# The first batch's filter in 74 small transfers beside x, and the weights behind x in one queue

## The chip, the cores and the metric

The kernel runs on one core of a Trainium2 chip. A core has five engines that run side by side: TensorE (PE: the matmuls, with PEld for its weight loads), VectorE (DVE), ScalarE (ACT), GpSimd (POOL) and SyncE (SP, which only issues transfers here). Transfers between the chip's memory and the on-chip memory are issued by SyncE, ScalarE or GpSimd, each in the order of its own program, and are carried out by 16 DMA engines that all the queues share. The metric is the device time in microseconds (us) from the first to the last instruction. It is taken as a median over runs, lower is better.

## The reference

A Fourier filter over the sequence, followed by a two-layer network with an ELU:

```python
def _attn_ref(x, filt_r, filt_i):          # x: (8, 3008, 256)
    X = np.fft.rfft(x, axis=1)             # 1505 frequencies
    Y = X * (filt_r + 1j * filt_i)[None]   # filt_r, filt_i: (1505, 256)
    return np.fft.irfft(Y, n=x.shape[1], axis=1)

def _moe_ref(x, w_in, w_out):              # x: (24064, 256)
    h = x @ w_in                           # (256, 2048)
    g = np.where(h > 0, h, np.exp(np.minimum(h, 0)) - 1)
    return g @ w_out                       # (2048, 256)
```

The two weights arrive as 64-bit floats: 2 x 256 x 2048 x 8 bytes are 8.4 MB. The filters are 32-bit: 2 x 1505 x 256 x 4 bytes are 3.08 MB. One batch of x is 3008 x 256 x 4 bytes, 3.08 MB.

## The kernel before

The sequence length is split as 3008 = 47 x 64. The work on one batch is a chain of small matrix products.

- *a*: 64-point transforms over one index. For batch 0 this is `a_first(c)` in six chunks c of four pairs of rows. It needs the chunk of x that `x_load_first(c)` brings (two transfers: 64 rows of 4 KB, and 64 times four runs of 1 KB) and a 256 KB piece of the table `tf`.
- *t*: `t_first(g)` brings the result of *a* into the layout that the next step wants, by transposing on TensorE. It needs `eye`. Batches 1 to 7 do this by a trip through memory.
- *b*: `b_unit(b, g)` for g = 0 to 7: the 47-point transforms on TensorE, then four products with the filter on VectorE (L312 to L315).
- *bi* and *y*: `bi_unit` and `y_write` are the inverse 47-point transforms and a trip through memory.
- *n*: `n_unit` is the last inverse transform. Its six pieces m per batch are the input rows of the network.

The network (`up_steps`, `down_steps`) takes each piece through four quarters of the 2048 hidden channels, with a seven-product scheme for 2 x 2 blocks, so that w_in and w_out are held in seven combinations per quarter (`w_in[q]`, `w_out[q]`).

The schedule is written out by hand. After a start-up stage, the loop over `items` (8 batches, 6 pieces, 4 quarters) interleaves the network of one batch with the Fourier steps of the next, by the table `plan`. Batch 0 has no earlier batch to hide behind. So the start-up stage has to do the whole Fourier chain of batch 0 up to `n_unit(0, 0)`, and also turn the 64-bit weights into 32-bit ones. This study is about that stage.

Each of 16 weight blocks k (512 KB) takes four calls: `w_fetch(k)` issues its transfer; `w_split(k)` (VectorE, L576 and L577) takes mantissa and exponent bits apart; `w_float(k)` (ScalarE, L582 to L587) makes floats of them; `w_join(k)` (VectorE, from L593) puts them together and, for every second block, forms the three extra combinations. The blocks share buffers with x and other tiles. Blocks 0 to 7 are worked on before the first `b_unit`, blocks 8 to 15 between the steps of *b* (`TICKS`).

The filter of batch 0 is one tile `ff`, 128 x 8192 floats, of which each `b_unit(0, g)` reads the part g. Row q of the first half-tile is a frequency 64 q + ..., so neighbouring rows of the tile lie 64 KB apart in memory, in runs of 2 KB or (mirrored, read backwards) of 1 KB. `ff` is zeroed first, since some entries get no data. Every transfer into `ff` brings all eight values of g for its rows. So the first product of `b_unit(0, 0)` waits for the last of them.

The transfers of the start-up stage before the change stand in two queues:

- SyncE: table piece and x chunk for c = 0 to 5, the tables `gr`, `gi`, `gf`, `eye`, then 11 transfers of filt_r (`f_read_first(ff, a, 0)`), then `gb` and a table for *n*.
- GpSimd: weight blocks 0 and 1, the zeroing of four tiles and of `ff`, then in the loop over c a one-element copy from x chunk c into `junk` (L670; it makes the queue wait until that chunk has landed) and weight block c + 2; after it 11 transfers of filt_i (`f_read_first(ff, a, 1)`), then weight blocks 8 to 13, and 14 and 15.

In the compiled program every queue has eight semaphores for its transfers, taken in turn. From the ninth on, a transfer is issued only when the one eight before it in the same queue has landed.

Of the kernel before, what the change touches and what calls it, by code (L numbers as in the profile page):

```python
# [10 lines left out]
FP32 = mybir.dt.float32  # L11
# [11 lines left out]
N1 = 47  # L23
N2 = 64
NF = N // 2 + 1
P = 128
D = 256
# [4 lines left out]
XC = 4  # L32
NXC = H // XC
NG = K2 // 4
# [3 lines left out]
HALVES = slice(0, 64), slice(64, 128)  # L38
# [67 lines left out]
def kernel(  # L106
# [9 lines left out]
    nc = tc.nc  # L116

    ta_d, tn_d, gb_d, gr_d, gi_d, tf_d, eye_d, gf_d = [
        nc.inline_tensor(t, name=n + "_t").ap()
        for t, n in zip(_make_tables(), ("ta", "tn", "gb", "gr", "gi", "tf", "eye", "gf"))  # L120
    ]

    def pool(name, bufs, **kw):
        return ctx.enter_context(tc.tile_pool(name=name, bufs=bufs, **kw))

    glob = pool("glob", 1)
# [17 lines left out]
    gb, gr, gi = (glob.tile([P, 2, 64], FP32, name=n) for n in ("gb", "gr", "gi"))  # L144
# [1 line left out]
    w_in, w_out = ([glob.tile([P, 7, 2, P], FP32, name="%s%d" % (n, i)) for i in range(4)] for n in ("wi", "wo"))  # L146

    fbufs = [glob.tile([P, 2, 2, D], FP32, name="f%d" % i) for i in range(FBUFS)]
    junk = glob.tile([P, 1], FP32, name="junk")
    edges = glob.tile([P, 2], FP32, name="edges")  # L150
    fd = fdp.tile([NG, 2, 48, 2, 2, D], FP32, name="fd")

    xs, tas, tns, t1s, t2s, ss, t3s, t4s, zs, yds, ys, g_of, po_of, cs_, sds = ({} for _ in range(15))

    def raw(src, row, ap, col=0):
        return bass.AP(tensor=src.tensor, offset=src.offset + row * D + col, ap=ap)
# [52 lines left out]
    zt = [[], [w[3].rearrange("p a b c -> p (a b c)") for w in (w_in, w_out)]]  # L209
    ROWS = 112  # L210

    def x_load_first(c):
        if c < XBUFS:
            t = xp.tile([P, 2, 2, D], FP32, tag="xc", name="xc").rearrange("p k u d -> p (k u) d")
        else:
            t = t1p.tile([P, XC, D], FP32, tag="t1", name="x1")
        if c < 2:
            w = tnp.tile([P, 4, P], FP32, tag="tn", name="tn")
        else:
            if c % 2 == 0:  # L220
                tas["pair"] = t4p.tile([P, 4, D], FP32, tag="t4", name="t0").rearrange("p u (w f) -> p (u w) f", f=P)
            w = tas["pair"][:, 4 * (c % 2):4 * (c % 2) + 4, :]
        xs[0, c], tas[0, c] = t, w
        nc.sync.dma_start(w, tf_d[:, 4 * c:4 * c + 4, :])
        nc.sync.dma_start(t[HALVES[0]].rearrange("p u d -> p (u d)"), raw(x, XC * c, [[N1 * D, 64], [1, XC * D]]))
        u = 1 if c == 0 else 0
        if u:
            nc.gpsimd.memset(t[HALVES[1], 0, :], 0.0)
        nc.sync.dma_start(t[HALVES[1], u:XC, :], raw(x, N1 - XC * c - u, [[N1 * D, 64], [-D, XC - u], [1, D]]))

    def a_first(c):
        xt, w = xs.pop((0, c)), tas.pop((0, c))
# [44 lines left out]
        for a, r in enumerate((LO, HI)):  # L277
            nc.gpsimd.dma_start(t[r].rearrange("p c u d -> p (c u d)"), fd[g, a].rearrange("q c u d -> q (c u d)"))

    def f_read_first(t, a, part):  # L280

        r = a * 64
        for src, c, queue in (((filt_r, 0, nc.sync), (filt_i, 1, nc.gpsimd))[part],):
            queue.dma_start(t[r:r + 24, :, c, :, :].rearrange("q g u d -> q g (u d)"),
                                raw(src, 2 * a, [[64 * D, 24], [4 * D, NG], [1, 2 * D]]))
            for u in range(2):
                g0 = 1 if a == u == 0 else 0
                for r0, n in ((24, 16), (40, 7)):  # L290
                    queue.dma_start(t[r + r0:r + r0 + n, g0:NG, c, u, :],
                                        raw(src, 64 * (r0 - 23) - 4 * g0 - 2 * a - u,
                                            [[64 * D, n], [-4 * D, NG - g0], [1, D]]))
            if a == 0:
                queue.dma_start(t[24:48, 0, c, 0, :], raw(src, 32, [[64 * D, 24], [1, D]]))

    def tile_mm(ps, table, k, rhs, special):
        for u, w, v in ((0, 1, 1), (1, 1, 0)) if special else ((0, 2, 0),):
# [44 lines left out]
    def tn_read(b, m):  # L343
        w = tns[b, m] = tnp.tile([P, 4, P], FP32, tag="tn", name="tn")
        nc.sync.dma_start(w, tn_d[:, 4 * m:4 * m + 4, :])
# [200 lines left out]
    def w_fetch(k):  # L546
        q, j = divmod(k, 4)

        if k in (3, 4):
            wd = t2p.tile([P, 4, D], FP32, tag="t2", name="wd").rearrange("p u d -> p (u d)")  # L550
        elif k in (10, 11):
            wd = t1p.tile([P, XC, D], FP32, tag="t1", name="wd").rearrange("p u d -> p (u d)")
        elif k in (6, 7, 8, 9, 15):
            wd = xp.tile([P, 2, 2, D], FP32, tag="xc", name="wd").rearrange("p k u d -> p (k u d)")
        else:
            wd = fbufs[{5: 0, 12: 1, 13: 2, 14: 0}.get(k, k)].rearrange("p c u d -> p (c u d)")
        wd = wds[k] = wd.bitcast(U32).rearrange("p (a w) -> p a w", w=2)
        if j < 2:
            srcs = [moe_w_in.bitcast(U32)[ts(j, P), ts(q, 1024)]]
        else:  # L560
            srcs = [moe_w_out.bitcast(U32)[ts(4 * q + 2 * (j - 2) + i, P), :] for i in range(2)]
        for i, s in enumerate(srcs):
            n = 512 // len(srcs)
            nc.gpsimd.dma_start(wd[:, ts(i, n), :].rearrange("p a w -> p (a w)"), s)

# [65 lines left out]
    with tc.manual_schedule():  # L633
# [3 lines left out]
        with tc.tile_pool(name="boot", bufs=1) as bp:  # L637
            ff = bp.tile([P, NG, 2, 2, D], FP32, name="ff")
            eye = bp.tile([P, P], FP32, name="eye")
            gf = bp.tile([P, 2, 64], FP32, name="gf")  # L640
            pq = [bp.tile([P, 2, D], FP32, name="pq%d" % i) for i in range(2)]
            zt[0] += [bp.tile([P, 16 * ROWS], FP32, name="zt%d" % i) for i in range(2)]

            for k in range(2):
                w_fetch(k)
            for c in range(NXC):
                x_load_first(c)
            wtmp.append([kp.tile([P, 512], U32, tag=t, name=n) for t, n in (("k0", "wm"), ("k1", "we"))] +
                        [kp.tile([P, 2, 512], FP32, tag="c", name="wfl")])
            wtmp.append([sdp.tile([P, 2, D], FP32, tag="sd", name=n).bitcast(U32).rearrange("p a b -> p (a b)")  # L650
                         for n in ("wm", "we")] +
                        [t1p.tile([P, XC, D], FP32, tag="t1", name="wfl").rearrange("p (a b) d -> p a (b d)", a=2)])
            for i, v in enumerate((1151.0 * 2 ** 23, 255.0 * 2 ** 23)):
                nc.vector.memset(edges[:, i:i + 1], v)
            for z in zt[0] + zt[1]:
                nc.gpsimd.memset(z.rearrange("p (k r) -> p k r", r=ROWS)[:, :, 48:64], 0.0)
            nc.gpsimd.memset(ff, 0.0)
            for t, d in ((gr, gr_d), (gi, gi_d), (gf, gf_d), (eye, eye_d)):
                nc.sync.dma_start(t, d)
            for a in range(2):  # L660
                f_read_first(ff, a, 0)

            def tick(k):
                w_float(k)
                w_join(k - 1)

            for c in range(NXC):
                w_split(c)

                nc.gpsimd.tensor_copy(out=junk[0:1], in_=xs[0, c][0:1, 0, 0:1])  # L670
                w_fetch(c + 2)
                w_float(c)
                a_first(c)
                if c > 0:
                    w_join(c - 1)
            for a in range(2):
                f_read_first(ff, a, 1)
            for k in range(NXC + 2, 14):
                w_fetch(k)
            for g in range(4):  # L680
                t_first(g)
            for k in range(NXC, 8):
                w_split(k)
                tick(k)
                w_fetch(8 + k)
            nc.sync.dma_start(gb, gb_d)
            tn_read(0, 0)
            for g in range(NG + 2):
                k = TICKS.get(g)
                if k:  # L690
                    w_split(k)
                if 2 <= g < NG - 2:
                    t_first(g + 2)
                if g >= 2:
                    bi_unit(0, g - 2)
                if g < NG:
                    b_unit(0, g, ff[:, g], gf, pq if g % 2 else None)
                if g >= 2:
                    y_write(0, g - 2, (nc.sync, nc.scalar if g == NG + 1 else nc.sync))
                if g == NG + 1:  # L700
                    y_read(0, 0, (nc.sync, nc.scalar))
                if k:
                    tick(k)
# [22 lines left out]
        for b in range(B):  # L726
            t = (b - 1) * PER
            if b > 0:
# [7 lines left out]
                for g in range(NG + 2):  # L736
                    s = t + 9 + g
# [6 lines left out]
                for g in range(NG):  # L744
                    s = t + 7 + g
# [11 lines left out]
        for i in range(-PER, len(items) + 3):  # L757
# [3 lines left out]
            for k in "UUDUDDU":  # L761
                s = ups if k == "U" else downs
# [4 lines left out]
            for k in "DUUDUDD":  # L767
                s = ups if k == "U" else downs
# [40 lines left out]
```

## Time and profile before

| | before |
|---|---|
| time, median of 3 | 2679.97 us (2678.12 to 2680.19) |
| profiled span | 2675.4 us |
| TensorE busy | 2597.6 us (97%) |
| VectorE busy | 1841.1 us (69%) |
| ScalarE busy | 1504.4 us (56%) |
| GpSimd busy | 252.2 us (9%) |
| first matmul of the last inverse transform of batch 0 (L363) | 125.5 us after the start |

TensorE is busy nearly all the time from about 126 us on. Before that it has gaps, and the rows of the profile that matter are those of the first 126 us: which transfer ends which wait, and how much the 16 DMA engines move in each stretch. A stretch's row gives the busy time of each engine and its count of instructions, the granted TensorE clock, the mean busy share of the DMA engines (transfers that overlap on one engine can take it above 1) and the GB/s moved.

### The profile page before, as it was taken

The numbers are of one execution on the slowest core, as the hardware profiler recorded it, in microseconds if no ns is written. First come the engines' busy times: TensorE is split into PE (matmuls) and PEld (weight loads), VectorE is DVE, ScalarE is ACT, GpSimd is POOL, SyncE is SP. The second block draws the span as 40 slices with busy tenths as digits, with TensorE's granted clock in tenths as the row PEclk, the third lists the DMA queues.
The fourth block names the chain that finished last, engine by engine and source line by source line (L and its number), as shares of the span: only waits on it lengthen the run. The fifth ranks groups of instructions, "written<-read, shape, count | busy, mean of one in ns | idle before, by whom it ended". The sixth has DMA issues, their size and how long they took to land.

```text
span 2675.4 us, 37291 instructions
## 1 busy us (share of the span) xinstructions
PE 2597.6 (97%) x13508; PEld 2213.8 (83%) x13508; DVE 1841.1 (69%) x3201; ACT 1504.4 (56%) x2621; POOL 252.2 (9%) x302
## 2 busy tenths in 40 slices
PE   3699999999999999999999999999999999999998
PEld 3388789887898878988789878898789887898887
DVE  3876766767766776767766776676767677666665
ACT  4565555655555555555555555555555555555554
POOL 3030200012000120002100021000210011000000
PEclk7799999999999999999999999999999999999999
DMA  9564421343114331343314233133421233110110
GB/s 194 145 143 100 112 50 38 90 104 97 38 45 120 86 85 35 82 104 79 77 43 102 73 97 75 38 85 97 103 56 38 73 83 85 38 40 19 22 26 16
DMA packets 230936, 202.87 MB, mean 76 GB/s; under 512 B 132952, under 2 KB 197579, under 8 KB 230753
## 3 DMA queue, kind: packets, MB, share of 16 engines
q1 hardware_dynamic: 213457, 164.84, 25.5%
q0 software_dynamic: 16992, 35.19, 5.5%
q8 instruction: 107, 1.75, 0.3%
q14 instruction: 76, 0.62, 0.1%
q10 hardware_dynamic: 304, 0.46, 0.1%
HBM read 128.45 MB, written 74.97 MB: 76 GB/s over the span
## 4 chain that ended last, share of the span: by engine, by line
PE 95%; DMA 3%; DVE 2%; ACT 0%; issue 0%; SPq 0%; POOL 0%; DVEq 0%; POOLq 0%; ACTq 0%
PE po L493 42%; PE phs L411 25%; PE phd L411 12%; PE pha L411 6%; PE psn L363 3%; PE pva L300 2%; PE psr L300 2%; PE psa L201 2%; DMA wd<-in_moe_w_out_dram 1%; DMA ff<-in_filt_i_dram 1%; DMA xc<-in_x_dram 1%; DMA tn<-tf_t 0%; PE pvb L300 0%; PE psa L236 0%; PE psi L300 0%
## 5 line engine op out<-in xcount | busy, mean ns | idle before, releaser
L493 PE MATMUL po<-g,wo 128*128 128x256 f32 (+1 forms) x5376 | 1297.1, 376 | 0.0
L493 PEld LDWEIGHTS po<-g,wo 128*128 128x128 f32 x5376 | 1016.7, 190 | 127.9 <-issue 16.2
L422 ACT ACTIVATE g<-phs 128x512 f32<-128x512 f32 (+1 forms) x576 | 338.7, 588 | 843.3 <-PE phs L411 842.6
L419 DVE TENSOR_TENSOR g<-phd,g 128x512 f32<-128x512 f32 (+1 forms) x384 | 259.4, 676 | 464.9 <-ACT e L429 278.7
L429 ACT ACTIVATE e<-e 128x512 f32<-128x512 f32 (+1 forms) x768 | 477.3, 621 | 24.3
L411 PE MATMUL phs<-y,wi 128*128 128x256 f32 (+1 forms) x1536 | 395.0, 380 | 0.0
L411 PE MATMUL phs<-ys,wi 128*128 128x256 f32 (+1 forms) x1536 | 387.8, 375 | 1.5 <-ACT g L422 1.5
L433 DVE SCALAR_TENSOR_TENSOR g<-e,g 128x512 f32<-128x512 f32 (+1 forms) x576 | 386.9, 672 | 0.2 <-ACT e L429 0.2
L428 ACT ACTIVATE e<-g 128x512 f32<-128x512 f32 (+1 forms) x576 | 352.9, 613 | 35.1 <-DVE g L419 29.0
L411 PEld LDWEIGHTS phs<-y,wi 128*128 128x128 f32 x1536 | 285.0, 190 | 82.7 <-ACT t L332 34.1
L411 PEld LDWEIGHTS phs<-ys,wi 128*128 128x128 f32 x1536 | 291.9, 190 | 34.8 <-ACT g L422 2.2
L433 DVE SCALAR_TENSOR_TENSOR g<-e,phs 128x512 f32<-128x512 f32 (+1 forms) x192 | 129.9, 677 | 138.4 <-ACT e L429 138.4
L411 PE MATMUL phd<-ys,wi 128*128 128x256 f32 (+1 forms) x768 | 194.0, 375 | 1.8 <-DVE g L419 1.8
L411 PE MATMUL pha<-y,wi 128*128 128x256 f32 (+1 forms) x768 | 193.9, 375 | 0.0
L411 PE MATMUL phd<-y,wi 128*128 128x256 f32 (+1 forms) x768 | 193.7, 375 | 0.0
L428 ACT ACTIVATE e<-phs 128x512 f32<-128x512 f32 (+1 forms) x192 | 112.9, 588 | 141.9 <-PE phs L411 141.0
L321 POOL TENSOR_TENSOR sr<-sr,sp 128x512 f32<-128x512 f32 x56 | 71.2, 1271 | 1242.8 <-DVE sp L314 1242.8
L411 PEld LDWEIGHTS phd<-ys,wi 128*128 128x128 f32 x768 | 145.9, 190 | 18.7 <-DVE g L419 2.5
L411 PEld LDWEIGHTS pha<-y,wi 128*128 128x128 f32 x768 | 146.0, 190 | 16.6 <-ACT y L365 0.2
L411 PEld LDWEIGHTS phd<-y,wi 128*128 128x128 f32 x768 | 146.1, 190 | 16.2
L473 DVE TENSOR_TENSOR g<-g,g 128x512 f32<-128x512 f32 (+1 forms) x192 | 130.7, 681 | 6.7
L470 DVE TENSOR_TENSOR g<-g,g 128x512 f32<-128x512 f32 (+1 forms) x192 | 130.7, 681 | 6.6
(141 smaller groups left out, 2403.0 us busy)
## 6 DMA issues: line engine op xcount, KB each, us to landing
yd<-t SPq DMA_DIRECT2D x127, 192.0 KB
t<-yd SPq DMA_DIRECT2D x190, 128.0 KB
z<-t SPq DMA_DIRECT2D x84, 256.0 KB
f<-fd POOLq DMA_DIRECT2D x112, 192.0 KB, 3.7
t<-z SPq DMA_DIRECT2D x224, 96.0 KB
out_dram<-o SPq DMA_DIRECT2D x640, 32.0 KB
tn<-tn_t SPq DMA_DIRECT2D x48, 256.0 KB
xc<-in_x_dram SPq DMA_DIRECT2D x84, 128.0 KB
```

Of the source, the lines that this page charges most:

```text
L300: nc.tensor.matmul(ps[:, u:u + w, :], table[k, v, :], r[k, u:u + w, :], start=n == 0, stop=n == len(rhs) - 1)
L321: nc.gpsimd.tensor_tensor(out=sr, in0=sr, in1=p, op=ALU.add)
L363: nc.tensor.matmul(ps[:, ts(q, P)], t[:, i - 4 * m, ds(dh * P, P)], w[:, i - 4 * m, :], start=True, stop=True)
L411: nc.tensor.matmul(ps[:, a, 0:h], w_in[q][:, COMBO[n], a, :], y[n], start=start and a == 0, stop=True, skip_group_check=True)
L419: nc.vector.tensor_tensor(out=g[o], in0=i0, in1=i1, op=ALU.add)
L422: nc.scalar.activation(out=g[o], in_=i0, func=AXT.Copy)
L428: nc.scalar.activation(out=e, in_=src, func=AXT.Relu, scale=-1.0)
L429: nc.scalar.activation(out=e, in_=e, func=AXT.Exp, scale=-1.0)
L433: nc.vector.scalar_tensor_tensor(out=g[n], in0=es[n], scalar=1.0, in1=src, op0=ALU.subtract, op1=ALU.max)
L470: nc.vector.tensor_tensor(out=b12, in0=b22, in1=b12, op=ALU.subtract)
L473: nc.vector.tensor_tensor(out=g["t4"], in0=g["b21"], in1=g["t2"], op=ALU.subtract)
L493: nc.tensor.matmul(po[i][:, u, 0:h], w_out[q][:, COMBO[n], a, :], g[n][:, a, :], start=q == 0 and a == 0 and n in (1, 3, 6, 4), stop=True, ...
```

## The change

The filter of batch 0 no longer waits behind x and the weights. It goes out from GpSimd's queue from the start, both filters, cut into pieces of four rows: 6 groups of rows x 2 half-tiles x 2 filters x 3 transfers, and 2 single ones, 74 in all where there were 22. GpSimd does not issue any weights any more. They go into SyncE's queue, between the chunks of x: x chunk, table piece, weight blocks, in the order in which they are needed. The `junk` copy that paced GpSimd's queue goes. `x_load_first` is split into `x_place_first` (which takes the buffers) and the issue of the transfers, and the table piece now follows its x chunk. Since GpSimd is to issue at once, `ff` is zeroed by ScalarE (one half) and VectorE (the other).

```diff
-    def x_load_first(c):
+    def x_place_first(c):
...
-        nc.sync.dma_start(w, tf_d[:, 4 * c:4 * c + 4, :])
-        nc.sync.dma_start(t[HALVES[0]].rearrange("p u d -> p (u d)"), raw(x, XC * c, [[N1 * D, 64], [1, XC * D]]))
+
+    def x_load_first(c):
+        t = xs[0, c]
         u = 1 if c == 0 else 0
         if u:
             nc.gpsimd.memset(t[HALVES[1], 0, :], 0.0)
+        nc.sync.dma_start(t[HALVES[0]].rearrange("p u d -> p (u d)"), raw(x, XC * c, [[N1 * D, 64], [1, XC * D]]))
         nc.sync.dma_start(t[HALVES[1], u:XC, :], raw(x, N1 - XC * c - u, [[N1 * D, 64], [-D, XC - u], [1, D]]))
+        nc.sync.dma_start(tas[0, c], tf_d[:, 4 * c:4 * c + 4, :])
...
-    def f_read_first(t, a, part):
...
-        r = a * 64
-        for src, c, queue in (((filt_r, 0, nc.sync), (filt_i, 1, nc.gpsimd))[part],):
-            queue.dma_start(t[r:r + 24, :, c, :, :].rearrange("q g u d -> q g (u d)"),
-                                raw(src, 2 * a, [[64 * D, 24], [4 * D, NG], [1, 2 * D]]))
-            for u in range(2):
-                g0 = 1 if a == u == 0 else 0
-                for r0, n in ((24, 16), (40, 7)):
-                    queue.dma_start(t[r + r0:r + r0 + n, g0:NG, c, u, :],
-                                        raw(src, 64 * (r0 - 23) - 4 * g0 - 2 * a - u,
-                                            [[64 * D, n], [-4 * D, NG - g0], [1, D]]))
-            if a == 0:
-                queue.dma_start(t[24:48, 0, c, 0, :], raw(src, 32, [[64 * D, 24], [1, D]]))
+    def f_read_first(t):
...
+        for q in range(0, 24, 4):
+            for a in range(2):
+                for c, src in enumerate((filt_r, filt_i)):
+                    r = 64 * a + q
+                    nc.gpsimd.dma_start(t[r:r + 4, :, c, :, :].rearrange("q g u d -> q g (u d)"),
+                                        raw(src, 64 * q + 2 * a, [[64 * D, 4], [4 * D, NG], [1, 2 * D]]))
+                    n = min(4, 23 - q)
+                    for u in range(2):
+                        g0 = 1 if a == u == 0 else 0
+                        nc.gpsimd.dma_start(t[r + 24:r + 24 + n, g0:NG, c, u, :],
+                                            raw(src, 64 * (q + 1) - 4 * g0 - 2 * a - u,
+                                                [[64 * D, n], [-4 * D, NG - g0], [1, D]]))
+        for c, src in enumerate((filt_r, filt_i)):
+            nc.gpsimd.dma_start(t[24:48, 0, c, 0, :], raw(src, 32, [[64 * D, 24], [1, D]]))
...
-            nc.gpsimd.dma_start(wd[:, ts(i, n), :].rearrange("p a w -> p (a w)"), s)
+            nc.sync.dma_start(wd[:, ts(i, n), :].rearrange("p a w -> p (a w)"), s)
...
-            for k in range(2):
-                w_fetch(k)
             for c in range(NXC):
+                x_place_first(c)
+            for c in range(3):
                 x_load_first(c)
+                for k in ((0, 1), (2,), (3,))[c]:
+                    w_fetch(k)
+            nc.scalar.memzero(ff[:, 0:NG // 2])
...
-            nc.gpsimd.memset(ff, 0.0)
-            for t, d in ((gr, gr_d), (gi, gi_d), (gf, gf_d), (eye, eye_d)):
-                nc.sync.dma_start(t, d)
-            for a in range(2):
-                f_read_first(ff, a, 0)
+            nc.vector.memset(ff[:, NG // 2:NG], 0.0)
+            f_read_first(ff)
...
             for c in range(NXC):
                 w_split(c)
-
-                nc.gpsimd.tensor_copy(out=junk[0:1], in_=xs[0, c][0:1, 0, 0:1])
-                w_fetch(c + 2)
                 w_float(c)
                 a_first(c)
                 if c > 0:
                     w_join(c - 1)
-            for a in range(2):
-                f_read_first(ff, a, 1)
-            for k in range(NXC + 2, 14):
+                if c + 3 < NXC:
+                    x_load_first(c + 3)
+                if c + 3 == NXC:
+                    for t, d in ((gr, gr_d), (gi, gi_d), (gf, gf_d), (eye, eye_d)):
+                        nc.sync.dma_start(t, d)
+                w_fetch(c + 4)
+            for k in range(NXC + 4, 14):
                 w_fetch(k)
```

More of the change, by code (lines that the diff above doesn't have):

```diff
@@ L148 @@
     fbufs = [glob.tile([P, 2, 2, D], FP32, name="f%d" % i) for i in range(FBUFS)]
-    junk = glob.tile([P, 1], FP32, name="junk")
     edges = glob.tile([P, 2], FP32, name="edges")
```

## The prediction

> **What bounds the kernel now.** I first looked at the busy shares by stage. The columns are: stretch in us, its length, busy us of PE, PEld, DVE, ACT, POOL, granted clock, DMA share, GB/s.
>
> ```profile
> 5.00:36.00 31.00, 16.37 (x80) 15.19 (x80) 17.07 (x35) 19.12 (x42) 13.87 (x19) 0.89 1.06 250
> 36.00:66.00 30.00, 10.23 (x76) 8.62 (x76) 8.91 (x18) 11.90 (x23) 8.98 (x16) 0.67 1.01 145
> 66.00:75.00 9.00, 0.00 (x0) 0.00 (x0) 1.25 (x3) 0.66 (x1) 3.22 (x6) 0.50 1.01 335
> 75.00:113.00 38.00, 34.80 (x197) 14.04 (x198) 36.86 (x74) 25.26 (x44) 0.52 (x1) 0.84 0.31 86
> 113.00:126.00 13.00, 2.45 (x16) 1.11 (x15) 9.88 (x21) 6.73 (x12) 0.00 (x0) 0.70 0.56 136
> 126.00:2675.00 2549.00, 2533.72 (x13144) 2174.87 (x13142) 1767.02 (x3053) 1439.42 (x2500) 221.78 (x250) 1.00 0.29 71
> ```
>
> The reader is to see three regimes. From 126 us TensorE is the bound (2533.7 of 2549 us) and nothing in the change touches that. From 75 to 113 us VectorE is (36.9 of 38 us): the filter products of batch 0 and weight blocks 8 to 15. Up to 75 us it is the DMA engines, whose share is about 1, and the compute engines stand still towards the end of it. In that part the rate is 250 GB/s while x and weights move, 145 while the filter moves, 335 once only weights are left.
>
> The waits of VectorE and the chain of waits say which transfer ends the stage:
>
> ```profile
> DVE sr L312 <- DMA ff<-in_filt_r_dram: 23.2, 1, 23.2
> ```
>
> ```profile
> 13.19 14.02 DMA xc<-in_x_dram
> ...
> 34.48 12.48 DMA wd<-in_moe_w_out_dram
> ...
> 47.24 16.84 DMA ff<-in_filt_i_dram
> ...
> 65.24 9.10 DMA wd<-in_moe_w_out_dram
> ...
> 74.35 0.68 DVE si L313
> ```
>
> VectorE is idle for 23.2 us and starts the first product (L312) at 73.75 us, released by a filt_r transfer of SyncE's queue. The chain names weights just before 74.35, but L313 reads no weights. GpSimd's timeline shows that filt_i was in before that:
>
> ```profile
> 53.99 0.58 POOL L291 DMA_DIRECT2D ff<-in_filt_i_dram  x1 [1.18 <-DMA ff<-in_filt_i_dram]
> 56.19 0.58 POOL L564 DMA_DIRECT2D wd<-in_moe_w_in_dram  x1 [1.61 <-DMA ff<-in_filt_i_dram]
> ...
> 68.43 0.53 POOL L564 DMA_DIRECT2D f<-in_moe_w_in_dram  x1 [0.42 <-issue]
> ```
>
> The last filt_i transfer leaves at 53.99 us. The issue at 68.43 waits for it (it is eight places on), so it landed by then. Its operands have long been ready: *b*'s first matmuls run at 44.9 us. So the start-up could be up to 73.75 - 50.5 = 23.2 us shorter at an unchanged later course, 50.5 us being where VectorE has finished weight block 6.
>
> [...] the share is about 1 from 5 to 75 us whichever queue feeds. So the change can gain from order, evenness and packet mix, not from a second road. [...]
>
> **The change part by part.**
>
> *Bytes.* Before the first product VectorE needs x (3.1 MB), six pieces of `tf` (1.5 MB), weight blocks 0 to 7 (4.2 MB), small tables (0.3 MB) and the whole filter (3.1 MB): 12.2 MB, the same before and after. Blocks 8 to 15 (4.2 MB) now come behind them. Before, blocks 8 to 10 and part of 11 to 13 came ahead of the end of the filter: in 0 to 74 us about 0.7 + 250 x 31 = 7.8 MB, 145 x 30 = 4.4 MB and 8 us at 335 = 2.7 MB were moved, 15 MB. So 2.8 MB leave the stage.
>
> *DMA time.* x, tables and weights, 9.1 MB, at the 250 GB/s of the first row: 36 us. The filter: if it moves at 145 GB/s even when spread out, 21 us; if it is only slow because much of it is in flight at once, and runs at 250 beside x, 12 us. With 2 us until the first bytes: 50 to 59 us. I take 57, since nothing in the trace shows the filter fast.
>
> *GpSimd's queue.* It can't issue before `ff` is zeroed. GpSimd's own zeroing of 8192 columns takes 6.92 us (3.94 to 10.86). ScalarE gets 4096 columns; its 512-column operations take about 0.6 us, so at most 4.8 us after the table load that ends at 2.03, thus 6.9 us. VectorE gets the other half from about 1 us; its 512-column operations take 0.42 us, so 3.4 us. Both are hidden: the first weights, which ScalarE and VectorE wait for, land at 9.2 us before, and now behind the first x chunk. GpSimd starts at about 6.5 us. One issue costs 0.53 to 0.58 us (L564 and the smaller L291), so 74 are 39 to 43 us. From the ninth on each also waits for the landing of the one eight before: 74 / 8 = 9.25 round trips. The trace bounds a round trip from both sides: 3.7 us is the median of f<-fd (192 KB, DMA share about 0.3), and 10.4 us is the median for the `fd` tile, whose transfers stand behind large ones. That makes 34 or 96 us. I estimate 3.2 us fixed (3.7 less 192 KB at 375 GB/s) plus the queueing: [...] That is 5.8 us, and 9.25 x 5.8 = 54 us. The filter is complete at about 6.5 + 52 = 58 to 60 us.
>
> *SyncE's queue.* x chunk 5 now stands behind 7.6 MB and its share of the filter. By the same rates it lands at about 45 to 49 us, later than before, where the last `a_first` starts at 36.28. From that start to *b*'s first matmul it took 44.88 - 36.28 = 8.6 us, so *b* is ready at 54 to 58 us. Block 7 lands near 57; `w_split(7)` and `w_join(6)` (0.84 and 2.1 us of VectorE) come before the first product: 60 us. Waits for buffers in the queue (block 5 for `w_join(0)`, 6 to 9 for `a_first(0)` to `(3)`) are over before their turn. Behind them stand only later blocks, `gb` and y_write, whose first issue was at 82 us.
>
> *Removed.* The `junk` copies and the pacing cost nothing but order.
>
> *Sum.* First product at about 60 us instead of 73.75. After it the same 52 us follow: VectorE is busy 36.9 of 38 us with unchanged work, and blocks 8 to 15 arrive at 335 GB/s, 1.6 us each, against 5 us per step that uses them. So the gain reaches the end one for one: 2680 - 14 = 2666 us.
>
> **Rivals.**
>
> *A, quicker.* The filter runs at x's rate when spread out, everything is there at 50 us, and the first product starts at 51 to 54: 20 to 23 us, 2657 to 2660. For it: 335 GB/s at the end shows headroom. Against: each GpSimd issue, 39 us at least, plus waits.
>
> *B, hidden or given back.* The round trip is 6.5 to 8 us, or x starves behind 4 KB filter packets: first product at 69 to 78 us, within 5 us of now, 2675 to 2685. For it: weights from GpSimd took 7 us to land at best.
>
> *C, slower.* [...] their round trip is near 10.4 us: complete at 6.5 + 96 = 102 us, and 28 us are lost: 2708. With 9 us it is 90 and 2696. For it: only a few rows per transfer, landings of 13.8 to 18.7 us for `ff` now. Against: those are of transfers five times as large behind half-megabyte blocks.
>
> **How the numbers follow.** My case, first product between 54 and 69 us: 0.65, of which I expect 60. A: 0.13. B: 0.10. C: 0.12. Faster is my case and A, 0.78. The range goes from 2655 (A with nothing lost) to 2684 (B), which leaves out C and a little beyond A.
>
> **What would show it.** Right: L312 first starts near 60 us, its wait is a few us, GpSimd's 74 issues end by about 55 us with under 0.3 us between most, GB/s is above 200 from 5 to 57 us, and from the first product to L363's first matmul there are 52 us as before. Wrong: GpSimd stands 0.5 us or more before most issues; the filter's last transfer is the releaser at over 70 us; x chunk 5 lands after 55 us; or the stage after the first product grows because blocks 8 to 15 come late.

## The result, and the profile after

The changed kernel takes 2716.3 us (median of 4 runs, 2714.7 to 2720.9), beside 2679.1 us for the kernel before on the same chip: a ratio of 1.0142, 95% interval 1.0124 to 1.0159. It is 37 us slower. The forecast was 2666 us.

First, the busy shares by stage of the changed kernel. The columns are those of the table in the prediction: stretch, length, busy us of PE, PEld, DVE, ACT and POOL with counts, granted clock, DMA share, GB/s.

```profile
5.00:15.00 10.00, 3.50 (x16) 3.34 (x16) 3.70 (x8) 6.66 (x13) 5.08 (x8) 0.90 1.02 253
15.00:65.00 50.00, 19.77 (x88) 18.58 (x89) 17.97 (x39) 16.89 (x38) 19.13 (x32) 0.57 1.11 155
65.00:95.00 30.00, 7.06 (x54) 5.59 (x52) 3.21 (x8) 9.40 (x17) 13.08 (x22) 0.61 1.07 171
95.00:110.00 15.00, 0.00 (x0) 0.00 (x0) 0.00 (x0) 0.00 (x0) 6.91 (x12) 0.50 0.35 51
110.00:149.00 39.00, 33.54 (x194) 13.89 (x195) 37.44 (x74) 25.28 (x44) 0.52 (x1) 0.84 0.24 61
149.00:163.00 14.00, 2.67 (x16) 0.94 (x16) 10.82 (x23) 6.89 (x12) 0.00 (x0) 0.76 0.54 127
163.00:2713.00 2550.00, 2534.45 (x13144) 2172.38 (x13144) 1766.96 (x3053) 1439.87 (x2500) 222.71 (x250) 1.00 0.29 71
```

The long TensorE stage is the same (2534.45 busy us of 2550, before 2533.72 of 2549), and so is the VectorE stage ahead of it. All that grew is the start-up: it lasted until 74 us before the change and now lasts until 110. In it the DMA share is as high as ever (1.11), but the rate is 155 GB/s where it had been 250 in the first 36 us. The engines are occupied and move less: a share of 1 doesn't say that bytes flow. From 95 to 110 us no compute engine does anything, and GpSimd issues 12 transfers.

The waits of the changed kernel name what is missing. The columns are engine, tile, line, releaser: us in total, times, longest.

```profile
DVE sr L315 <- DMA ff<-in_filt_r_dram: 36.0, 1, 36.0
...
POOL ff L294 <- DMA ff<-in_filt_r_dram: 33.3, 18, 5.0
...
POOL ff L294 <- DMA ff<-in_filt_i_dram: 17.9, 14, 2.7
```

VectorE stands 36.0 us before its first product (L315, which was L312) and is released by the filter. Ahead of that GpSimd itself stands for its own transfers' landings, 33.3 + 17.9 us over these 32 issues. The chain of waits (start, us, what) shows how landing follows landing:

```profile
5.99 0.78 POOL ff L289
6.77 9.88 DMA ff<-in_filt_r_dram
...
16.93 11.51 DMA ff<-in_filt_i_dram
...
29.42 12.74 DMA ff<-in_filt_r_dram
...
92.20 12.42 DMA ff<-in_filt_r_dram
...
107.17 3.23 DMA ff<-in_filt_r_dram
```

GpSimd begins at 5.99 us. Then one transfer of 10 to 13 us after another lies on the chain, each of which lets GpSimd issue the one eight places on. The part on issues says the same (out<-in, engine, operation, count, KB each, median us from issue to landing):

```profile
ff<-in_filt_r_dram POOLq DMA_DIRECT2D x12, 64.0 KB, 12.2
...
ff<-in_filt_r_dram POOLq DMA_DIRECT2D x15, 32.0 KB, 11.8
```

A piece of 64 KB lands in 12.2 us, and one of half the size in 11.8. The median of all 74 is 11.5 us, and 74 / 8 x 11.5 = 106 us, which from the first issue at 6 us on leads to 112; VectorE was released at 110.

The timelines show the other operands of the first product (start, us, engine, line, what, in brackets the idle time before it and its releaser):

```profile
56.39 3.76 PE L238 MATMUL psa<-t,x 128*128 128x128 f32 x16 [6.76 <-DMA t<-tf_t]
...
67.53 0.43 DVE L579 TENSOR_SCALAR wm<-wd 128x512 uint32<-128x512 uint32 x1 [2.13 <-DMA wd<-in_moe_w_out_dram]
...
110.49 0.69 DVE L315 TENSOR_TENSOR sr<-psr,ff 128x512 f32<-128x512 f32 x1 [35.97 <-DMA ff<-in_filt_r_dram]
```

The last `a_first` starts at 56.39 us (before 36.28), weight block 7 is split at 67.53, and VectorE has no more to do at 74.5. So x and weights are late too, by 20 us in the case of x. That lateness is hidden: VectorE is through with it 36 us before the filter is there. From the first product to *n*'s first matmul it takes 52.4 us (162.9 - 110.5; before 51.7). The 36.7 us lost by the first product reach the end one for one.

### The profile page after: what moved, and what is told of

It reads as the page before. It is cut to its first block, busy times and chain, and to the rows that moved or that the text cites. A ratio compares the mean times of both kernels' runs of the same rounds, so it can differ in the third digit from the quotient of the medians.

```text
span 2713.3 us, 37327 instructions
## 1 busy us (share of the span) xinstructions
PE 2601.0 (96%) x13508; PEld 2214.7 (82%) x13508; DVE 1843.5 (68%) x3202; ACT 1509.2 (56%) x2622; POOL 269.0 (10%) x334
## 4 chain that ended last, share of the span: by engine, by line
PE 93%; DMA 4%; DVE 2%; ACT 0%; issue 0%; POOL 0%; DVEq 0%; ACTq 0%
PE po L496 42%; PE phs L414 24%; PE phd L414 12%; PE pha L414 6%; PE psn L366 3%; DMA ff<-in_filt_r_dram 2%; PE pva L303 2%; PE psr L303 2%; PE psa L200 2%; DMA ff<-in_filt_i_dram 1%; DVE si L316 0%; DVE sr L315 0%; PE pvb L303 0%; DMA t<-yd 0%; DVE wfl L598 0%
## 5 line engine op out<-in xcount | busy, mean ns | idle before, releaser
L414 PEld LDWEIGHTS phd<-y,wi 128*128 128x128 f32 x768 | 145.8, 190 | 16.5
```

The source lines that it names most:

```text
L414: nc.tensor.matmul(ps[:, a, 0:h], w_in[q][:, COMBO[n], a, :], y[n], start=start and a == 0, stop=True, skip_group_check=True)
```

## The experiments

The filter's pieces land slowly. Four theories were to be told apart: that each transfer has a long fixed round trip, whatever its shape; that the pitch or scattering of the rows read slows them; that a piece of four neighbouring rows is too narrow, in the number of its rows ('narrow' in the expectations) or in the partitions that it writes ('port'; no view shows engines or ports of a piece, so both names are guesses); and that the order in SyncE's queue is what hurts. Some kernels below ran once only. The kernel before took 2668 to 2683 us in the runs made beside the experiments, so a single time says little about a difference of less than 15 us; the landings in its trace say more.

### Cut along g instead of along rows

Each piece now takes as many rows as the kernel before (24, 16 or 7) and two of the eight g. There are 82 of them, of 38 KB in the mean where the 74 have 42.

```diff
-        for q in range(0, 24, 4):
+        for p in range(0, NG, 2):
...
-                    nc.gpsimd.dma_start(t[r:r + 4, :, c, :, :].rearrange("q g u d -> q g (u d)"),
-                                        raw(src, 64 * q + 2 * a, [[64 * D, 4], [4 * D, NG], [1, 2 * D]]))
+                    nc.gpsimd.dma_start(t[r:r + 24, p:p + 2, c, :, :].rearrange("q g u d -> q g (u d)"),
+                                        raw(src, 4 * p + 2 * a, [[64 * D, 24], [4 * D, 2], [1, 2 * D]]))
...
```

> The changed kernel with its filter cut the other way: all 24 (16, 7) rows per transfer, but two of the eight values of g; 82 transfers of about the same size instead of 74. Theory 'narrow' [...]: the median landing falls from 11.5 us to 4 to 6 us, GpSimd issues nearly back to back, and the last filter piece lands at 55 to 65 us. Theory 'round trip' (under this load a landing takes about 11.5 us whatever the shape, and eight in flight set the rate): median landing stays at 10 to 13 us and the last piece lands at 82 / 8 x 11.5 + 6 = 124 us. Theory 'pitch' (reads 64 KB apart are slow in themselves): nothing gained or worse, 110 us or later, since now up to 24 rows of that pitch are read by one transfer. The first product needs only the pieces of its own g here, so its start alone decides nothing; the landings do.

It took 2664.5 us, ratio 0.9959 (0.9944 to 0.9974): faster than the kernel before. Its issues and its stretch from 25 to 65 us:

```profile
ff<-in_filt_r_dram POOLq DMA_DIRECT2D x8, 96.0 KB, 7.3
...
ff<-in_filt_r_dram POOLq DMA_DIRECT2D x15, 32.0 KB, 6.7
```

```profile
25.00:65.00 40.00, 25.95 (x151) 21.43 (x153) 23.82 (x50) 25.56 (x52) 24.93 (x45) 0.76 0.99 255
```

96 KB over 24 rows land in 7.3 us where 64 KB over four take 12.2. So the time isn't fixed per transfer, nor set by the bytes of a piece. The last pieces still leave only at 76.4 us, later than expected. The first product starts at 57.8 us all the same: it reads only its own g, which lands first. Two things changed at once here, the shape of a piece and the order in which the filter comes; the run with rows spread out, below, has the first alone.

### Eight rows a piece, and the old 22 pieces

```diff
-        for q in range(0, 24, 4):
+        for q in range(0, 24, 8):
...
-                    n = min(4, 23 - q)
+                    n = min(8, 23 - q)
```

> The changed kernel with pieces of eight rows, 38 transfers instead of 74. 'Round trip': the landing stays near 11.5 to 13 us, the filter is complete at 38 / 8 x 12 + 6 = 63 us, the first product at about 70 to 76 us (then weight block 7 decides), time near 2680 us. 'Narrow': [...] about the same, 60 to 65 us. 'Pitch': bytes decide, complete at 100 us or later, time near 2710 us.

The other run has the pieces of the kernel before (24, 16 and 7 rows, all g), but all from GpSimd's queue at the start:

```diff
-        for q in range(0, 24, 4):
-            for a in range(2):
-                for c, src in enumerate((filt_r, filt_i)):
-                    r = 64 * a + q
+        for a in range(2):
+            for c, src in enumerate((filt_r, filt_i)):
+                r = 64 * a
...
```

> The changed kernel with the filter in the old 22 pieces (24, 16 and 7 rows), all from GpSimd's queue from the start; the rest of the change stays. 'Round trip' and 'narrow': complete at 40 to 60 us, the first product at 65 to 75 us, time 2670 to 2682 us: the cut alone made the kernel slower. 'Pitch': complete at 90 us or later, time 2695 us or more. If x and the weights are what the early filter costs, weight block 7 lands at 67 us or later all the same.

Eight rows: 2691.6 us, ratio 1.0061 (1.0037 to 1.0085). Pieces of twice the size land in 12.7 us (median), hardly more than those of four rows, so the last leaves at 63.0 us instead of 107.7. The time is about 12 us above what was expected, since the first product starts only at 83.8 us: x and weights had become the later of the two (the last `a_first` at 68.3 us, weight block 7 split at 76.3). Old pieces: 2679.3 us, ratio 1.0015 (1.0008 to 1.0022). All 22 are issued by 39.1 us and land in 13.8, and the first product, at 72.1 us, again comes behind x and weights (last `a_first` at 60.4). So the cost of filter transfers beside x isn't only their own time, it is also what they do to x. From 25 to 65 us the run with eight rows moved:

```profile
25.00:65.00 40.00, 11.25 (x48) 10.46 (x48) 10.30 (x23) 11.41 (x24) 13.04 (x23) 0.59 1.08 149
```

### The side that is read: pitch and scattering

The first run reads the rows 63 KB apart instead of 64, the second takes a row's eight runs from one contiguous stretch. Both multiply batch 0 with other frequencies of the filter; transfers, sizes and destinations are as in the changed kernel.

```diff
-                                        raw(src, 64 * q + 2 * a, [[64 * D, 4], [4 * D, NG], [1, 2 * D]]))
+                                        raw(src, 63 * q + 2 * a, [[63 * D, 4], [4 * D, NG], [1, 2 * D]]))
...
```

> The changed kernel with its 74 pieces, but the rows of the filter of batch 0 are read 63 KB apart instead of 64 KB, so that batch 0 is multiplied with other frequencies; sizes, counts and order are unchanged. 'Pitch': the median landing falls from 11.5 to 6 us or less, the rate in 25 to 65 us rises from 150 to 220 GB/s or more, the filter is complete at 50 to 65 us, time 2665 to 2680 us. 'Narrow' and 'round trip': landing 10.5 to 12 us, complete at 100 to 108 us, time within 5 us of 2716.

```diff
-                                        raw(src, 64 * q + 2 * a, [[64 * D, 4], [4 * D, NG], [1, 2 * D]]))
+                                        raw(src, 64 * q + 2 * a, [[64 * D, 4], [2 * D, NG], [1, 2 * D]]))
...
```

> The changed kernel with its 74 pieces, but the eight runs of a row are read from one contiguous stretch (step 2 KB or 1 KB instead of 4 KB), so that batch 0 is multiplied with other frequencies; destinations, sizes and counts are unchanged. If the scattered reading in memory is what makes a four-row piece slow, its landing falls from about 12 us (64 KB pieces) to 7 or 8. 'Narrow' [...]: 11 to 12.5 us as before, filter complete at 100 to 109 us.

2712.7 us (ratio 1.0143, 1.0122 to 1.0164) and 2716.9 us (one run); first product at 106.7 and 112.2 us, landings of 11.0 and 11.9 us. Neither matters: the 64 KB pitch is cleared, as far as a change to 63 KB can clear it.

### The order without the filter

This kernel has no filter transfers for batch 0; its filter stays zero.

```diff
     def f_read_first(t):
-        for q in range(0, 24, 4):
...
+        pass
```

> The changed kernel without any filter transfer for batch 0 (its filter stays zero). It shows what x and the weights take in SyncE's queue alone. If the early filter is what holds them up: above 230 GB/s from 5 to 45 us, the last first-step matmul group begins at 34 to 42 us instead of 56.4, weight block 7 is taken at 40 to 48 us instead of 67.5, the first product starts at 48 to 56 us, time 2652 to 2665 us. If the new order in SyncE's queue is itself slow: the group begins after 50 us and the time stays above 2670.

2651.6 us (one run). The last `a_first` starts at 33.2 us, the first product at 45.9. Its windows:

```profile
15.00:25.00 10.00, 6.00 (x35) 5.58 (x36) 7.00 (x15) 7.84 (x18) 0.00 (x0) 1.00 1.07 280
25.00:35.00 10.00, 7.75 (x47) 7.20 (x46) 7.68 (x17) 6.83 (x16) 0.00 (x0) 0.66 0.99 282
```

x and weights alone run at 280 GB/s at the same DMA share. The order in SyncE's queue is innocent. Putting the filter back as in the change adds its 3.1 MB and takes the total down to 155 GB/s.

### Same pieces, rows spread out

Here a piece still has four rows, the same bytes and the same place in the queue, but its rows lie six apart: rows q, q+6, q+12, q+18, each in another group of four partitions. The count stays 74.

```diff
-        for q in range(0, 24, 4):
+        for q in range(6):
...
-                    nc.gpsimd.dma_start(t[r:r + 4, :, c, :, :].rearrange("q g u d -> q g (u d)"),
-                                        raw(src, 64 * q + 2 * a, [[64 * D, 4], [4 * D, NG], [1, 2 * D]]))
+                    nc.gpsimd.dma_start(t[r:r + 19:6, :, c, :, :].rearrange("q g u d -> q g (u d)"),
+                                        raw(src, 64 * q + 2 * a, [[6 * 64 * D, 4], [4 * D, NG], [1, 2 * D]]))
...
```

> The changed kernel with its 74 pieces of four rows, but each piece takes four rows that stand six partitions apart instead of four neighbours; the result is the same. 'Port' [...]: landing falls from 12 us to 8 or less, filter complete by 75 us. 'Narrow' [...]: unchanged, 11 to 12.5 us, complete at 100 to 109 us.

2684.4 us (one run), 32 us less than the changed kernel. Its issues, the stretch from 25 to 65 us of the changed kernel and then its own, and its first product:

```profile
ff<-in_filt_r_dram POOLq DMA_DIRECT2D x12, 64.0 KB, 7.8
...
ff<-in_filt_r_dram POOLq DMA_DIRECT2D x15, 32.0 KB, 7.5
```

```profile
25.00:65.00 40.00, 15.58 (x71) 14.52 (x71) 14.41 (x33) 13.03 (x29) 14.38 (x24) 0.54 1.11 149
```

```profile
25.00:65.00 40.00, 17.19 (x108) 14.87 (x108) 14.71 (x32) 20.65 (x42) 23.98 (x41) 0.71 1.08 259
```

```profile
76.55 0.69 DVE L313 TENSOR_TENSOR sr<-psr,ff 128x512 f32<-128x512 f32 x1 [22.63 <-DMA ff<-in_filt_r_dram]
```

12.2 us have become 7.8, the total is 259 GB/s instead of 149 in the same stretch, and the last `a_first` comes at 40.4 us. Only which rows share a piece was changed, so it isn't their number that makes a piece slow. The last piece leaves at 74.6 us, hardly earlier than with the cut by g (76.4), where the first product started at 57.8: these 19 us come from the order, on top of what the shape gains.

### Which end, and how far

Spreading moves both the rows read and the partitions written. The next two do one each, and so put other frequencies into batch 0's filter: the first writes partitions six apart from neighbouring rows, the second reads rows six apart into neighbouring partitions. The third spreads both by two, so that four rows lie in two groups of four partitions.

```diff
-                                        raw(src, 64 * q + 2 * a, [[6 * 64 * D, 4], [4 * D, NG], [1, 2 * D]]))
+                                        raw(src, 64 * 4 * q + 2 * a, [[64 * D, 4], [4 * D, NG], [1, 2 * D]]))
...
```

> As the run with spread rows, but only on the side of the on-chip memory: a piece writes four partitions six apart and reads four neighbouring rows of the filter, 64 KB apart, as the changed kernel does. Rows land in other places, so that batch 0 is multiplied with other frequencies. 'Port' [...]: 64 KB pieces land in 7 to 8.5 us, time 2680 to 2690 us. 'Memory spacing' (rows 384 KB apart read faster than rows 64 KB apart): 11 to 12.5 us, 2710 to 2720 us.

```diff
-                    r = 64 * a + q
-                    nc.gpsimd.dma_start(t[r:r + 19:6, :, c, :, :].rearrange("q g u d -> q g (u d)"),
+                    r = 64 * a + 4 * q
+                    nc.gpsimd.dma_start(t[r:r + 4, :, c, :, :].rearrange("q g u d -> q g (u d)"),
...
```

> The counterpart: a piece reads filter rows 384 KB apart and writes four neighbouring partitions; rows land in other places, so that batch 0 is multiplied with other frequencies. 'Port': 11 to 12.5 us, 2710 to 2720 us. 'Memory spacing': 7 to 8.5 us, 2680 to 2690 us.

```diff
-        for q in range(6):
+        for q in (0, 1, 8, 9, 16, 17):
...
-                    nc.gpsimd.dma_start(t[r:r + 19:6, :, c, :, :].rearrange("q g u d -> q g (u d)"),
+                    nc.gpsimd.dma_start(t[r:r + 7:2, :, c, :, :].rearrange("q g u d -> q g (u d)"),
...
```

> The changed kernel with its 74 pieces, each of four rows two partitions apart, so that a piece covers two groups of four partitions instead of one (and the run with spread rows four); the result is the same. 'Port': between the two, 64 KB pieces at 8.5 to 10.5 us, filter complete at 80 to 95 us, time 2690 to 2706 us. If neighbours alone matter, not groups: 7 to 8.5 us, as with six apart.

(These diffs are against the kernel with rows six apart.) One run each: 2684.3, 2714.0 and 2693.1 us. First the written side spread, then the read side, then both by two:

```profile
25.00:65.00 40.00, 17.56 (x111) 15.34 (x110) 16.58 (x36) 21.20 (x43) 22.85 (x39) 0.76 1.08 249
```

```profile
25.00:65.00 40.00, 14.89 (x64) 13.94 (x64) 13.79 (x31) 13.59 (x30) 14.61 (x25) 0.62 1.11 150
```

```profile
25.00:65.00 40.00, 23.42 (x124) 20.88 (x124) 16.90 (x37) 22.29 (x45) 21.20 (x36) 0.63 1.08 223
```

The written side carries nearly all of it: 249 GB/s, 7.9 us to landing for 64 KB and a first product at 77.4 us. With the read side spread it is 150 GB/s, 11.3 us and 109.5 us, nearly as if nothing had been done. Two groups give most of the gain: 223 GB/s, 8.5 us and 84.3 us.

### Versions that keep the idea

The kernel before, with its filter cut by two g, in order of g on both queues, and weight blocks 8 to 11 between the pieces:

```diff
...
-            for a in range(2):
-                f_read_first(ff, a, 1)
-            for k in range(NXC + 2, 14):
+            for p in range(0, NG, 2):
+                f_read_first(ff, p, 1)
+                w_fetch(NXC + 2 + p // 2)
+            for k in range(NXC + 6, 14):
```

> The kernel before with its two queues and its order, but the filter in pieces of two values of g with all rows (41 per queue), in the order of g, and weight blocks 8 to 11 between them in GpSimd's queue. If pieces by g are what gains, and not the early start beside x: x as before (last first-step group at about 36 us), the first product at 50 to 58 us, time 2655 to 2668 us. If the 41 small pieces of SyncE's queue hold up the filter: products wait inside the later stage and the time is 2668 to 2680 us.

And the kernel cut by g from above, whose first two g are issued at once and the others when the last x chunk has landed:

```diff
...
-            f_read_first(ff)
+            f_read_first(ff, (0,))
...
+                if c == 5:
+                    nc.gpsimd.tensor_copy(out=junk[0:1], in_=xs[0, c][0:1, 0, 0:1])
+                    f_read_first(ff, (2, 4, 6))
```

> The changed kernel with pieces by g and all rows, of which the first two values of g go out at once and the other six only when the last chunk of x has landed (by a one-element copy on GpSimd). If the filter's share of the DMA engines is what still holds up x and the weights in the run with pieces by g: last first-step group at 34 to 40 us instead of 44.5, first product at 48 to 54 instead of 57.8 us, time 2654 to 2660 us. If not: within 3 us of 2664.

2657.4 us (ratio 0.9926, 0.9904 to 0.9947) and 2661.6 us (0.9928, 0.9912 to 0.9945). The intervals overlap: the two can't be told apart, and both beat the kernel before and the changed one. The second missed what was expected of it: its last `a_first` starts at 42.3 us (34 to 40 expected) and its first product at 55.4 (48 to 54). So holding six g back helped x little. The first's timeline:

```profile
49.79 0.69 DVE L310 TENSOR_TENSOR sr<-psr,ff 128x512 f32<-128x512 f32 x1
```

49.8 us, 4 us from the kernel without filter transfers (45.9). This kernel has the old queues, and its filter still stands behind x: it gets as much as any other without the early start. What the start-up of 74 us needed was small pieces cut by g, in the order in which they are used.

## Why the prediction was wrong

**The step that failed: "GpSimd's queue".** The form of its sum was right. Eight transfers are in flight (GpSimd's ninth issue, at 16.03 us, comes after 4.97 us of waiting for a landing), and 74 / 8 landings follow one another. The term "round trip" was mis-sized: 5.8 us estimated, 11.5 measured. That moves the filter's end from 60 to 110 us. The measured landing lies even above the upper bound that I named, 10.4 us and a time of 2708, and rival C has the right sign and almost the size. I set it aside because its landings were those of transfers five times as large. The runs show that bytes were the wrong measure: 32 and 64 KB over four rows, and 128 KB over eight (13.5 us), land in about the same time, and 96 KB over 24 rows in less. The fixed part of the estimate, 3.2 us, was about right: spread pieces of 64 KB issued after 60 us, four of the six when SyncE's queue had run empty, land in 3.2 us (filt_r) and 3.0 us (filt_i, medians of three). What it left for the queueing, 2.6 us (5.8 - 3.2), measured about 8.3 (11.5 - 3.2).

**What stands in its place.** The 2.6 us were my estimate; how many engines a piece of four rows occupies, no view shows. The estimate went by the number of rows and left out where they are written. A piece of `f_read_first` writes four neighbouring partitions, from a multiple of four on (only the last two transfers are wider). I call four such partitions a group. Six pieces in a row (two filters, one straight and two mirrored pieces each) write rows q to q+3 and q+24 to q+27, two groups, so that eight in flight write three or four. The 3.1 MB from 6 to 110 us are 30 GB/s.

That it matters where a piece writes is shown by the runs with only one end spread: 249 GB/s and 7.9 us with the written side six apart, 150 GB/s and 11.3 us with the read side. The size of a group, four, is less certain. With groups of eight, rows two apart would share one as neighbours do, yet they land in 8.5 us and not in 12.2. With groups of two, rows two apart would count like rows six apart, and 8.5 and 7.8 us, from one run each, hardly speak against that. What is scarce behind a group isn't shown: no view shows the way into the on-chip memory, or which engines carry a piece. The packets in the trace of the changed kernel show a delay, not its place. From 100.33 to 100.83 us, with filter pieces alone under way, four packets of 4 KB run side by side and take 568 to 648 ns each, four times the 159 ns that 31 of the 101 such packets from 98.4 to 110 us take. They may share something; a single engine that works on four packets in turn could look the same.

**What the wider pieces add.** Groups touched are not enough: the old pieces write up to six groups at once, and beside them the total is as low as beside pieces of four rows. Here are 10 us of the run with the old pieces and of the one cut by g, whose pieces have the same rows:

```profile
15.00:25.00 10.00, 3.61 (x16) 3.45 (x16) 0.00 (x0) 1.91 (x5) 2.85 (x5) 0.54 1.06 150
```

```profile
15.00:25.00 10.00, 4.06 (x17) 3.82 (x18) 4.36 (x9) 4.49 (x10) 6.07 (x11) 0.50 1.08 221
```

What sorts all the runs is how much one piece brings to each group of four partitions (the straight pieces of filt_r):

| run | rows, groups | KB to each group | landing, us | all queues, 15 to 40 us, GB/s |
|---|---|---|---|---|
| changed kernel | 4, 1 | 64 | 12.2 | 165 |
| read side spread | 4, 1 | 64 | 11.3 | 157 |
| eight rows | 8, 2 | 64 | 13.5 | 162 |
| old 22 pieces | 24, 6 | 64 | 13.2 | 167 |
| two apart | 4, 2 | 32 | 8.5 | 204 |
| six apart | 4, 4 | 16 | 7.8 | 236 |
| written side six apart | 4, 4 | 16 | 7.9 | 227 |
| cut by g | 24, 6 | 16 | 7.3 | 229 |
| no filter | | 0 | | 279 |

This was read off afterwards, and no run was made for it. The old pieces and the cut by g also differ in order and in bytes in flight.

How much of the 50.5 us (110.5 - 60) is this? With the rows spread the first product starts at 76.55, so 34 us are due to neighbouring partitions (in one run). The other 16.5 stay: even spread pieces land in 7.4 us (median) rather than 5.8, and 74 / 8 x 7.4 + 6 = 75. So 74 pieces by rows would have gained nothing even so: 2684 is in rival B's 2675 to 2685.

**It isn't x alone that holds the filter up.** When SyncE's queue has run dry, the pieces in flight in the changed kernel are alone, and still move slowly; those of the spread one don't. First the changed kernel, then the spread one:

```profile
98.00:101.00 3.00, 0.00 (x0) 0.00 (x0) 0.00 (x0) 0.00 (x0) 1.20 (x2) 0.50 0.35 41
101.00:104.00 3.00, 0.00 (x0) 0.00 (x0) 0.00 (x0) 0.00 (x0) 2.33 (x4) 0.50 0.28 32
```

```profile
70.00:74.00 4.00, 0.00 (x0) 0.00 (x0) 0.00 (x0) 0.00 (x0) 4.00 (x8) 0.50 0.28 65
```

At about the same DMA share, 32 to 41 GB/s against 65; and in the spread kernel GpSimd is busy all of the 4 us, so that issuing is its limit there. But the other queue has a large part in a landing. The changed kernel's three 64 KB pieces issued after 98 us land in 4.2 to 6.8 us, where 12.2 was the median. How the 11.5 us divide between the pieces ahead in the own queue and the other queue was not measured.

**"DMA time" and "SyncE's queue" failed too, beside the same pieces.** I took 250 GB/s for x and weights and expected the last x at 45 to 49 us and block 7 near 57; they came at 56 and 67. The kernel without filter transfers moved the same queue at 280. With the filter, which moves 30 GB/s itself, the total of all queues is not higher but 125 GB/s lower. The DMA share was 1.11 at 149 GB/s, and 1.08 at 259 with the rows spread: beside pieces of neighbouring rows the engines were as occupied and moved less. How such a piece holds up the other queue's transfers was not shown. Behind the filter this loss was hidden. In the runs with eight rows and with the old pieces it is what ends the start-up. One sum in "Bytes" is low: its terms make 15.5 MB, as the profile before has it (209 GB/s over 74 us), not 15. The forecast didn't use it.

**What was right.** GpSimd started at 5.99 us (6.5 expected), and the zeroing by ScalarE (3.6 us) and VectorE (3.5 us) was over before the first weights came at 8.9; only GpSimd's first issue waited for it, as reckoned. An issue took 0.59 us, a little more than the 0.53 to 0.58 assumed. The course after the first product was unchanged at 52 us, so the difference went through one for one, with the other sign.

**Open.** The large pieces of the kernel before also bring 64 KB to each group. That its 145 GB/s have the same cause is likely but wasn't tried by itself. Nor was a queue with more than eight in flight.

## What to carry to other kernels

Cut a transfer along the dimension in which its consumer takes it, and let no piece heap its bytes on few neighbouring partitions: here such a piece was slow itself (12.2 us beside 7.8 for the same 64 KB six apart), and all queues together moved less beside it (149 beside 259 GB/s). Many partitions alone didn't mend that, as the old pieces show (24 rows, 167 GB/s); many partitions with little for each did (24 rows cut by g, 229 GB/s). For a train of small transfers, count / in flight x landing is the time (here 74 / 8 x 11.5 = 106 us, and about 104 measured), and the landing has to come from a piece of the same shape beside the same traffic, not of the same bytes. And when the DMA share is 1, read the GB/s beside it before calling the engines full: 1.11 went with 149 GB/s, 1.08 with 259.

## What was unexpected of the hardware

- Four rows of the same bytes land in 12.2 us in neighbouring partitions, in 8.5 us two apart and in 7.8 us six apart; from where they are read makes little difference (11.3 us).
- A filter stream of 30 GB/s, shaped this way, brought the total from 280 to about 150 GB/s, at a DMA share of 1.11 where it had been 0.99 to 1.07.
- Spread pieces of 64 KB issued after 60 us, most of them when the other queue had run empty, landed in 3.0 to 3.2 us (medians) instead of 7.8: more than half of a landing came with the traffic beside it.
- Pieces of 4, 8 and 24 rows that bring 64 KB to each group of four partitions all held the total to 157 to 167 GB/s; with 16 KB to each group it was 227 to 236.
